# A retention layer with an MLP mixer on one core: another reserve behind crossbar turns, and another order of operations and loads

## The chip, the core and the metric

The kernel runs on one core of a Trainium2 chip. The core has five engines that run side by side, each with its own queue of instructions in fixed order: TensorE (PE in the profile; PEld is its loading of weights), VectorE (DVE), ScalarE (ACT), GpSimd (POOL) and SyncE (SP). Data goes between the device's memory (DRAM) and the core's memory (SBUF) by DMA, which POOL, SP and ACT issue; matmuls write into eight banks of accumulators (PSUM). The metric is the time of one execution on the device in microseconds (us).

## The reference

Two layers follow each other. For 4 batches, 8 heads, 768 steps and a head width of 64, a state decays by a factor of its head at each step and takes in an outer product; the output reads it with q. Then an MLP mixes along the steps, and another along the channels:

```python
def _attn_ref(q, k, v):
    gamma = 1.0 - 2.0 ** (-5.0 - np.arange(H))
    for t in range(S):
        state = gamma[None, :, None, None] * state + np.einsum('bhd,bhe->bhde', k[:, :, t], v[:, :, t])
        y[:, :, t] = scale * np.einsum('bhd,bhde->bhe', q[:, :, t], state)

def _moe_ref(x, w_tok1, w_tok2, w_ch1, w_ch2):
    xt = x.transpose(0, 2, 1)
    h = np.maximum(xt @ w_tok1, 0.0) @ w_tok2
    u = x + h.transpose(0, 2, 1)
    h2 = np.maximum(u @ w_ch1, 0.0) @ w_ch2
    return u + h2
```

x is the first layer's output with the heads side by side, (4, 768, 512). w_tok1 is 768 x 256, w_tok2 256 x 768, w_ch1 512 x 1536, w_ch2 1536 x 512. The output is float32.

## The kernel before

The recurrence is computed in six chunks of 128 steps: inside a chunk by masked score products, between chunks by a state that is carried on. The work falls into a front for each batch b and each of its four pairs of heads p, and a back for each batch.

**Front (function `front`).** q, k and v of a pair are loaded by POOL with a cast to float16 (the first k comes by SP in float32). k, and in batches 2 and 3 also q, is scaled with the head's decay (`decayed`, L533 on ACT or L535 on DVE, in two halves). Then both are turned, so that the head's width lies on the partitions (`turn`). A table named TURNS says how, for k, q and the result u: in batches 0 and 1 by PE (L557 for q, L559 for k, L792 for u) with a copy out of the bank by ACT or DVE; in batches 2 and 3 by the crossbar, which is a DMA with transpose that SP issues (L547 for k and q, L782 for u). After the turns, PE forms the chunk states (L589), which DVE carries on (L599, L601) and ACT scales (L619); it forms the scores (L640), which fill four banks and which DVE masks (L650); and it multiplies them with v (L670) and the states with q (L696). ACT casts the result (L712), PE runs the first MLP with the weights wt1 (L727) and wt2 (L747) with a relu between (L736 on ACT or L738 on DVE), and ACT casts u and keeps a float32 copy X (L712).

**Back (functions `widen`, `widen7`, `narrow`, `narrow7`).** With the turned u of all four pairs (the tile uT) and the weights wc1, PE forms the wide products. In batches 0 and 1 `widen` does it in a plain way (L826), with a relu by ACT alone (L842). In batches 2 and 3 `widen7` uses seven products in place of eight (L895), with sums of u (L865), copies (L906) and adds (L915); its six blocks begin with the products p1 and p2, which are the first to need uT. Then the narrow products with wc2 (L1044 and L1054 in the scheme of seven, L970 in the plain one) go through copies (L1034) and adds to X (L1061, L979), and the rows of X go out by a DMA that SP or ACT issues (L1087, L985).

**What sets the order.** Nothing is issued in the order of the source. All steps are recorded as `Op`s with the engines that they may run on, a planned cost for each and their dependences; `arrange` then plays the whole program through with those costs, a model of the DMA queues (`Rings`), the eight banks and the numbers of buffers. When an engine is free, it takes the first operation in its list that is ready. The list's order is given by `PRECEDENCE`, a string of two letters for each operation, found by a search outside of the kernel. The instructions are then emitted in the planned order, each engine's queue for itself; semaphores hold back whatever is early. Loads are requested in the order of the list `ORDER` at the end of the function (q00 is q of batch 0, pair 0; t1 and t2 are wt1 and wt2, a0 to a3 the pieces of wc1, b0 to b2 those of wc2), all on POOL's queue and at most a few at a time.

An operation may carry a guard. It counts in one place of `arrange`, where the time is worked out at which an operation may start:

```python
                x += (25 if eng[d.n] == e and d.dma is None else SEM) + o.guard
```

d is what the operation waits for and x is d's planned end. So a guard is a reserve in the plan alone: the operation is planned at least that many nanoseconds after the end of what it depends on, and so other work is planned ahead of it. No instruction comes of it. Before the change, every matmul step of the fronts of batches 1 to 3 has a guard of 200, and the steps of the back have none.

In the first 21 us of the plan, PE's holes of over 400 ns are partly filled with matmuls of zeros (fillers, L1164), as many as 0.7 of the planned hole divided by 165 ns (240 ns in the first two microseconds).

Of the kernel before, what the change touches and what calls it, by code (L numbers as in the profile page):

```python
# [89 lines left out]
def arrange(ops, BUFS, BANKS, rank):  # L90
# [181 lines left out]


PRECEDENCE = (
    "0b0900040a0105070c020d03060e080f230g272428250h260i382i373i2h330j2l342k2j350k2m29362n2a2o2b0l533m543h2c0m5543"
    "2d44560n472e3l3j2f453k2g460o393n482p2q3o2r0p3a492s3b4a3c3d4b4c3e4d4h3f0q4e4k574f4j3g0r2t584g3q4n2u4p3p4i4r3r"
    "4l0s2v4m3s5i2y2w3t5l2z0t2x5m593u31305a4o0u5b634q643v324s5h3w5c3y0v5k4t3x5d3z5j650w4u5e854066675f86415g5o0x5n"
    "4y7273425p765q4v5r68740y5s694w755t4z6a0z6b4x6c5u516d5077105v526h946e5y5w95116fhp5x6l5zhs6j6g12616khm606i62hj"
    "6n6mhnhkhqhthl6o6p13id6qighrihhuie146ri7iii8ifiaibi96shoicja81jb151z82i1i46ti52083i66x84hv21hwhy16hx22hz6ui0"
    "j46vi26ziy6wij6yiki317j570jjiljdje71jljkj8jcizj7jmjf7gj6181vj0iminj9is7jioit197hb0kb7iiuiv7kip1wiqa2jga3jh1x"  # L280
    "iwir7mji7l1y78ixjn1akc8779joju7a1b887b9089j17cjvj2911cjs7d8aj38b7ejp8c1dk5jtjy7fjqk78djw1ejz8eb17ojr7n8fk6jx"
    "7p968hk17q8j9z928ikga0k28g93k47rk0a1ax8l8nkr8k7s8mk9k8ay1fa4978o7wkska7tkt1gbva5k3khke7u98b28pku1hkk7va6997x"
    "a78qkdazkfkl7yki9abwa89bkv8ra9bxkjaa9c8skmab9ekw8vkp9g8tknct9f9h8wl09dko9i9j8xkqkx7z8u80cu9ll2kyl1kzadacl39k"
    "ah9n9ml6af9o8yael4cvl78zagaiakl59paml8ajal9q1ib3anlbc1byb49ub59rc21jbzb6aoc3b79sc4c0b8l99vc5c6ap9w9xla9tmqat"
    "lc9ybbaqc7benab9bdnbm1arbcm2c8bfm3ldasbgleaumsbacwmdawmeavmtcxbimmlfmncymfbhbjmpbk1klvmublma1lmrmblwmcmy1mlx"
    "mzn1ncn7n01nczmon2d0n8d1n31obmd2n9d3lsd4bnmvd5m7drboltd6dsm8dtbrlulpbplym9lzbqmjm0mwdumkd7mxmllqdblgepd8m4bs"
    "lmd9lrlnbudabtm5dclodec9m6dvddcanjeqcbdwlhdgccdfn4licdevdhernkceescgn5ewexcfcicheyn61pdxezljcjf0dyoretdz1qe0"
    "f1lke1ckosf2eue21rmgllmhclndnhe31sminfcpnicmnee41tdinlcnngnm1ucqolcoo5csomdjcrnoonnnoodko6opdlnpnqdmoqe5nrot"
    "oue6e9nse8dne7gloyntdoowgmovnudqnvdpoxfqf3nzoznxeafrecf4gnp3fno0p0fof7fseef6ebedgoo3f5efp4f9fbgpo1f8p6faego4"
    "p1fcnwo2ftfdnygreho7o8fugsgqfvelgtfwo9eigufxoap7fggyofpbp5oifjfhejfpgvocekp8emobfeodpaeoenoegwfffyp9gxohfzp2"  # L290
    "ogpcg1okfipsg5ojfkpgg4ptpdfmq9flg3puphg2pxg0pjpvqqpypepipkpwq0pfpzplq1pqpmpnq2prpoq7g7q4q8q3qbppqaq5qsr7qcqr"
    "qeq6g6qdqvqfqtqxqwqhsxquqgqig8qygaroqjqzqoqkg9qlr0qpr5gbqmr2r6ter9r1qnr8rer3rvrarcrprqr4rbrdrtrrgcrursrfgdrw"
    "rgs9rxrhrmrys3rnrjrirzs4gigerkghgfthtdggrls0tftjtigkgjs1svtgtms2tkgzs5tnsbtlsah3tqh0h1trh2tosys7h4h6h5tph7h8"
    "sgs6h9sctss8hashtttvsdhbtusetwhcsrtysksfssswhfsthdt0szheslt2hgsut1hihhsit3t4sjt6smt5snspt7t9t8tztbu3tauku4u0"
    "umtculu5u1u8u2upu9uauntxuqvpsoubu7ussqu6xqucurutuoviuduiuuv3ujufueuvuwugv1vzuxvjvkuhuzv2uyvlvnv0v6v4vow1vmwi"
    "v7v5vqv9vrv8vawgvsvxvbvgvyvuvtvcvhvdvvwny5vew0w6vwwhvfydw2w4wlwjw5y6w3wmwkytw7wow8x1wpw9wewqwvwfwbwawrwwwswc"
    "yuxnwty7wdwuy8xjy9wxxoyaxkx2xpxlxmxsyvxuwyxtwzx6x0xwxvx7xrxyybxxx8ycxzy1y0xax9y3y2xcy4xbx3xdywxeyxyyygyfxfx4"
    "xhyhyeyzx5z0xgyiypxiymylynyjyoyqykyrys"
)


# [1 line left out]
def kernel(  # L303
# [73 lines left out]
    def one(eng, cost, emit):  # L377
        return [(eng, cost[0], cost[1], emit)]
# [125 lines left out]
    def front(b, p):  # L504
# [22 lines left out]
        def decayed(tag, src, dep, g, hard):  # L527
# [12 lines left out]
            return dst, got  # L540
        K, kl = decayed("k16", KF, kd, gk, (b, p, "k") in HARD)

# [180 lines left out]
        def emit():  # L723
            acc = tile_of(T1, [P, 512], FP)
            for jt in range(NJ):
# [3 lines left out]
        t1 = op(one("PE", (672, 830), emit), x_ops + [wops["t1"], t2_done.get(b * NP + p - 1)],  # L729
                [T1], [X16])  # L730
# [11 lines left out]
        for j in range(2):  # L742
# [12 lines left out]
            t2 = op(one("PE", (335, 500), emit), [hr, wops["t2"], x_ops[j]], [], [H1, Y[j]])  # L755
# [50 lines left out]
    def back(b):  # L806
# [42 lines left out]
        def widen7():  # L849
# [3 lines left out]
            def u(k, half):  # L853
                return lambda: UT.tile[:, k * C2:(k + 1) * C2, half]
# [16 lines left out]
            def block(i):  # L871
# [6 lines left out]
                def weights(j):  # L878
                    if j < 4:
                        return lambda ct: AS.tile[:, j, ct, i * P:(i + 1) * P]  # L880
                    k, m = (j - 4) % 2, (j - 4) // 2
                    f = (i + m * M2) * P
                    return lambda ct: wc1[:, k * C2 + ct, f:f + P]

                def product(R, left, right, deps, first, extra):
                    opens = not lead

                    def emit():
                        if opens:
                            for x in H2s:  # L890
                                tile_of(x, [P, NF, SH], F16)
                        acc = tile_of(R, [P, 512], FP) if first else R.tile
                        r = right()
                        for ct in range(C2):
                            nc.tensor.matmul(acc[:, :SH], left(ct), r[:, ct], start=first and ct == 0,  # L895
                                             stop=ct == C2 - 1, skip_group_check=True)
# [200 lines left out]
        for f in steps:  # L1097
# [99 lines left out]
```

## Time and profile before

| what | value |
|---|---|
| time, median of 3 runs | 190.7 us (189.74 to 190.97) |
| the profiled execution | 190.58 us |
| its span, first to last instruction | 188.8 us |
| granted clock of TensorE | 1.0 |
| fillers (L1164) | 37 |
| crossbar turns on SP (L547, L782) | 24 |
| data moved by DMA | 24.92 MB |

The page's shares are averages over stages that have different limits: in the first 20 us the loads arrive one by one, later the engines limit each other. So the wait that ends last in a stage is looked for in that stage, by the timeline of an engine, by the table of busy times in stretches, and by the chain of waits, which goes back from the last instruction to what released each step. A row of the timeline gives start and length in us, the engine, the source line, the operation, the tiles and their shapes, how many instructions it merges, and in brackets the idle time ahead of it with what ended it. A matmul's length in such a row is longer than its share of PE's time, since matmuls overlap; the pace is read from the distance of starts.

### The profile page before, as it was taken

Reading aid. Unit: us, or ns where it says so; the run is one execution under the profiler, and the core shown is the slowest. Engines: PE = TensorE matmul, PEld = TensorE weight load, DVE = VectorE, ACT = ScalarE, POOL = GpSimd, SP = SyncE. Lnnn points to the kernel's source line nnn. Section 1 sums busy time; section 2 is a strip of 40 time slices with the busy share of each in tenths; the row PEclk is TensorE's granted clock in tenths of the full one; section 3 lists DMA queues with packets and bytes.
Section 4 is the critical chain, followed back from the end, with each engine's and each line's share of the span. In section 5 each row is a group of like instructions: output and inputs, shape, how many; then the busy total and the mean of one; then the engine's idle time right before and its main releaser. Section 6 shows DMA issues by size and latency. Waiting matters only on the chain.

```text
span 188.8 us, 5281 instructions
## 1 busy us (share of the span) xinstructions
PE 180.6 (96%) x2107; PEld 136.5 (72%) x2107; DVE 147.0 (78%) x398; ACT 145.7 (77%) x332; POOL 52.9 (28%) x62
## 2 busy tenths in 40 slices
PE   7977999999999999999899999999999999999993
PEld 3454898676688888866577988966678995656892
DVE  5588899455999988722078979989879978977972
ACT  7767899899979999999999979797884273766200
POOL 8995565634063604603016400000000000000000
PEclk9999999999999999999999999999999999999999
DMA  6999999999999999999999999683002044100044
GB/s 117 156 165 198 177 177 201 196 204 187 157 124 147 171 190 129 216 141 188 111 102 119 160 142 163 166 233 71 2 2 45 18 135 172 56 0 3 0 168 167
DMA packets 91977, 24.92 MB, mean 132 GB/s; under 512 B 81968, under 2 KB 89008, under 8 KB 91952
## 3 DMA queue, kind: packets, MB, share of 16 engines
q0 software_dynamic: 67456, 13.18, 92.0%
q1 hardware_dynamic: 24496, 11.41, 29.3%
q8 instruction: 16, 0.26, 0.7%
q14 instruction: 9, 0.07, 0.1%
HBM read 26.74 MB, written 6.29 MB: 175 GB/s over the span
## 4 chain that ended last, share of the span: by engine, by line
PE 73%; DMA 13%; ACT 5%; DVE 3%; POOL 3%; issue 1%; DVEq 0%; SPq 0%; POOLq 0%
PE bank L895 14%; PE bank L1044 13%; PE bank L826 11%; PE bank L1054 10%; DMA qT<-q 5%; PE bank L727 5%; PE bank L747 4%; DMA k<-in_k_dram 3%; PE bank L640 3%; PE bank L970 3%; PE bank L670 3%; DMA uT<-u 2%; PE bank L696 2%; PE bank L589 2%; DMA kT<-k 1%; PE bank L792 1%
## 5 line engine op out<-in xcount | busy, mean ns | idle before, releaser
L650 DVE TENSOR_TENSOR am<-bank,mask 128x384 f16<-128x384 f32 x64 | 32.0, 550 | 7.7 <-PE bank L640 7.7
L826 PE MATMUL bank<-uT,wc 128*128 128x384 f16 x192 | 35.6, 326 | 0.2 <-ACT X L712 0.2
L494 POOL DMA_DIRECT2D v<-in_v_dram x16 | 16.4, 1026 | 42.9 <-PE bank L696 19.6
L826 PEld LDWEIGHTS <-wc 128*128 128x128 f16 x192 | 17.7, 98 | 10.0 <-issue 0.5
L842 ACT ACTIVATE h<-bank 128x384 f16<-128x384 f32 x48 | 21.6, 518 | 1.5 <-PE bank L826 1.1
L1034 ACT COPY us<-bank 128x256 f32<-128x256 f32 x33 | 12.4, 381 | 12.8 <-PE bank L1044 12.7
L915 DVE TENSOR_TENSOR h<-bank,us 128x384 f16<-128x384 f32 x36 | 18.8, 552 | 4.3 <-ACT us L906 3.8
L906 ACT COPY us<-bank 128x384 f32<-128x384 f32 x36 | 16.4, 481 | 7.2 <-PE bank L895 5.2
L1044 PEld LDWEIGHTS <-hs 128*128 128x128 f16 x198 | 18.5, 98 | 2.3
L1061 DVE TENSOR_TENSOR X<-X,bank 128x256 f32<-128x256 f32 x44 | 17.8, 415 | 2.2 <-PE bank L1054 2.1
L619 ACT ACTIVATE cross<-U,gp 64x320 f16<-64x320 f32 x32 | 17.6, 560 | 2.5 <-DVE U L601 2.1
L1044 PE MATMUL bank<-wsum,hs 128*128 128x256 f16 x132 | 17.7, 273 | 0.0
L601 DVE SCALAR_TENSOR_TENSOR U<-U,gp,bank 128x64 f32<-128x64 f32 x64 | 16.2, 276 | 1.1 <-DVE U L599 0.2
L494 POOL DMA_DIRECT2D k<-in_k_dram x15 | 15.4, 1032 | 4.4 <-DMA wc<-in_moe_w_ch_dram 1.9
L712 ACT CAST x<-bank 128x384 f16<-128x384 f32 x32 | 14.8, 483 | 2.0 <-PE bank L696 1.9
L712 ACT CAST u<-bank 128x384 f16<-128x384 f32 x32 | 15.1, 488 | 1.1 <-PE bank L747 0.9
L533 ACT ACTIVATE k<-k,gk 128x384 f16<-128x384 f16 x24 | 14.3, 617 | 1.9 <-DMA k<-in_k_dram 1.8
L712 ACT COPY X<-bank 128x384 f32<-128x384 f32 x32 | 15.5, 496 | 0.1
L747 PE MATMUL bank<-h,wt 128*128 128x128 f16 x192 | 14.8, 219 | 0.0
L895 PE MATMUL bank<-hs,late 128*128 128x384 f16 x72 | 14.3, 326 | 0.0
L1054 PEld LDWEIGHTS <-h 128*128 128x128 f16 x132 | 12.7, 98 | 1.9
L1061 DVE TENSOR_TENSOR X<-X,us 128x256 f32<-128x256 f32 (+1 forms) x22 | 12.2, 554 | 2.4 <-ACT us L1034 1.9
(83 smaller groups left out, 355.3 us busy)
## 6 DMA issues: line engine op xcount, KB each, us to landing
out_dram<-X SPq DMA_DIRECT2D x23, 256.0 KB, 2.4
q<-in_q_dram POOLq DMA_DIRECT2D x16, 192.0 KB, 9.8
v<-in_v_dram POOLq DMA_DIRECT2D x16, 192.0 KB, 8.3
k<-in_k_dram POOLq DMA_DIRECT2D x15, 192.0 KB, 7.3
wc<-in_moe_w_ch_dram POOLq DMA_DIRECT2D x5, 512.0 KB, 13.5
wt<-in_moe_w_tok_dram POOLq DMA_DIRECT2D x2, 384.0 KB, 9.5
wc<-in_moe_w_ch_dram POOLq DMA_DIRECT2D x2, 256.0 KB, 9.2
us<-in_k_dram SPq DMA_DIRECT2D x1, 384.0 KB, 3.5
```

Source lines behind the costliest of these rows:

```text
L494: (nc.sync if hard else nc.gpsimd).dma_start(out=tile_of(s, [P, 2, NC, D], FP if hard else F16), in_=src.rearrange("h (c p) d -> p (h c) d ...
L619: nc.scalar.activation(r, u, AF.Copy, scale=g)
L650: nc.vector.tensor_tensor(am, SC[g].tile[:, :m * P].rearrange("p (i t) -> p i t", t=P), mask.to_broadcast([P, m, P]), ALU.mult)
L712: (nc.scalar.copy if e == "ACT" else nc.vector.tensor_copy)(tile(), t)
L747: nc.tensor.matmul(Y[j].tile[:, 2 * i * D:2 * (i + 1) * D], wt2[:, jt, t], H1.tile[:, jt], start=False, stop=(jt == NJ - 1), skip_group_ch ...
L826: nc.tensor.matmul(acc[:, :SH], wc1[:, ct, ft * P:(ft + 1) * P], UT.tile[:, ct, sh * SH:(sh + 1) * SH], start=(ct == 0), stop=(ct == NP - 1))
L842: nc.scalar.activation(H2.tile[:, ft], A.tile[:, :SH], AF.Relu)
L895: nc.tensor.matmul(acc[:, :SH], left(ct), r[:, ct], start=first and ct == 0, stop=ct == C2 - 1, skip_group_check=True)
L915: nc.vector.tensor_tensor(h(m, sh), R.tile[:, :SH], KS.tile[:, j], ALU.add)
L1044: nc.tensor.matmul(acc_[:, lo], l[:, j], r[:, j], start=first and j == 0, stop=j == K2 - 1, skip_group_check=True)
L1054: nc.tensor.matmul(acc_[:, lo], l[:, j], r[:, j], start=first and j == 0, stop=j == K2 - 1, skip_group_check=True)
L1061: (nc.vector if e == "DVE" else nc.gpsimd).tensor_tensor(dst(), dst(), b_(), ALU.add)
```

## The change

A constant RESERVE = (1500, 900) is added. The score products (L640) of the pairs whose q is turned by the crossbar, which are those of batches 2 and 3, get a guard of 1500 in place of 200. The products p1 and p2 of the first block of `widen7`, in batches 2 and 3, get a guard of 900 in place of none. PRECEDENCE is another string in the whole, and ORDER another list of loads. Computation, tiles, buffers, banks and the ways of turning are the same.

```diff
@@ PRECEDENCE @@
-    "0b0900040a0105070c020d03060e080f230g272428250h260i382i373i2h330j2l342k2j350k2m29362n2a2o2b0l533m543h2c0m5543"
...
+    "0f0j4f0e0c24272q250h2j2826373801032sa40b05070g00040d0a08092302064d0i29492l2k0k2m2n2o2a2b350l44362c452d0m3h46"
...
@@ before the operations are recorded @@
+    RESERVE = (1500, 900)
     HARD = {(0, 0, "k")}
@@ front: the scores @@
             a2 = op(one("PE", (k_, k_ + 155), lambda f=emit, r=run: f(r)), [kt, qt, two_before],
                     [SC[g] for g in run], [KT, QT], tiled="high")
+            a2.guard = RESERVE[0] if TURN[b, p, "q"] == "x" else a2.guard
             score_ops.update({g: a2 for g in run})
@@ widen7: block i @@
                 p2 = product(R3, weights(5), u(1, lo), ready + cw, True, [UT])
+                p1.guard = p2.guard = RESERVE[1] if i == 0 else 0
                 out_of(R3, 0, p2, k1, 0, 0)
@@ the loads @@
-    ORDER = ("q00 k00 q01 k01 v00 k03 k02 q02 v01 v02 q03 t1 t2 v03 k10 q12 q10 k11 v10 q11 q13 a1 a0 a3 "
-             "k12 a2 b1 b2 b0 q21 q20 v11 v12 k13 v20 v21 v13 k20 k21 k22 k23 v22 q22 q23 v23 k30 v30 q30 "
+    ORDER = ("q00 k00 q01 v00 k01 k02 k03 v01 v02 q02 q03 t1 t2 v03 k10 q12 q10 k11 q13 q11 a0 v10 a1 v11 "
+             "a3 a2 b1 b2 b0 k12 v12 k13 v20 v13 k20 q20 q21 v21 k21 k22 k23 v22 q22 q23 v23 k30 v30 q30 "
              "k31 v31 q31 v33 v32 k33 q32 k32 q33").split()
```

In the built program the counts of instructions change in a few places, by the planner's choice between engines: PE has 34 fillers for 37; ACT has 42 instructions of L533 for 41 and 16 of L736 for 15, and 5 copies of L572 for 6; DVE has 6 of L535 for 7, none of L738 for one, and 3 of L572 for 2; three output transfers of L1087 are issued by ACT instead of SP, 19 stay on SP for 22. The source lines from the score products on are one to three higher than before.

More of the change, by code (lines that the diff above doesn't have):

```diff
@@ L274 @@
 PRECEDENCE = (
-    "0b0900040a0105070c020d03060e080f230g272428250h260i382i373i2h330j2l342k2j350k2m29362n2a2o2b0l533m543h2c0m5543"
[L276 to L298, printed above, removed]
+    "0f0j4f0e0c24272q250h2j2826373801032sa40b05070g00040d0a08092302064d0i29492l2k0k2m2n2o2a2b350l44362c452d0m3h46"
@@ new lines @@
+    "3i3j54433m2e532f0n473f392g343k553a3l564e3n5m483b3c2r3o332h2i4a3d2u4p4b0q3e4c0o3g4h2p3q0p4k574j3r0r584g2t3s4n"
+    "4r5i0s2v5l2w4i2z4m0t2x4l593t3u315a2y5b634q4o640u3v324s5h403w3y5c0w5j4t5f5d3z5k650v5s4u5ohm5e4130665n3x4y425g"
+    "850x677273865p5r4v3p5q0y74684w504z755t0z164x95515u76946h521077625vhj5w6k5y115x6jhs5z6l606i126169hp6a6b6m136n"
+    "6chqht6dhnhk6ehlij6f797aikimhr7b7cin1h6g14ip7diqho6ohu6pi7iljejd6qi8ioidirie156rig1zhvifhwi9ia207eibhx6s217f"
+    "ici122jfi26tiyi3iz6xj06u787g6v17i47i6wi56y7jihi6hy7khz6z7h70iij1i07m71j2181vjnj3jjis19ja811w7lj482j51xjojb1a"
@@ new lines @@
+    "j67njgjc1y837piv841biwjljpixjk9087jm1cit9188jhjqiu7o89j7jrjij81d8a7qkb8bj98cjs8dk51e9zjukck6jt8e8fk77rjwjva2"
+    "8ha3jy7uk8jx8jb08ik1jz7sb18gkga0k28la1k08kk48m921faxkh8nk9kray7tkt93kkksaz7wku8okvkaklb5b67vkdb2969e8p8wa5kw"
+    "97ke7x98a6bvk3998qa79i7ya89bl0kfa98raa9ckil19dbwbx8sab9akj9g8t7z9hac9fknl4l5ctkm9k8u9mkokpb38v80cu9jkq9lb41i"
+    "l99nkxb78xla8y9ob8kyb9kz8z9pl2l39ql6agcvbyah9rbz9ul7n69sc0aeajal9v9tl8c1c29w9xlbc39ybbc4aic5akbfljamlkc6bemd"
+    "anmebcc71jldbdaoc81kbhbjcwlemacx1l1gn4mbn5cyaplflcbaadll1mbgbiatbkm1m2mc1nmjblmkm31om7mlm8aqm9lsarmfafltmnau"
@@ new lines @@
+    "msasbmawluavn2bnmmdrbodzezcmdhn3brdsn1czmomtdtd0bplvlmd1mud2bqd3lzd4bslpd5mylybtlwm0mzlglxlhd6duc9d7lilqcbn0"
+    "m4lndvcam5lrccdwn7locdepn8ewm6eqbumvcfd9chmwn9erd8njesmxdaceetdb1pmpnanecgdddccinhng1qcjdfnknfmqninb1rmrnleu"
+    "ckevnc1scldxdeexo5nddgeydy1tf0e0cne1f11uo6noe2nnmge3npf2nqnmmhe4cpnrnsmicodiolcqntopcscrongloromgmnunvdjgnfq"
+    "oooso3frdknwoqnxoynzdnfnnye5otdlo0oufso4e9dmo8e7ove8dodpe6fof3oxo2ozf5gop0gpf6dqeaf7ecp3f4eeebedpkftf9p4efo7"
+    "fbo1fpp6grp1egfuf8gsfvfap2ehocfzfwp5gtfdeifxguelfyodgqp7fcoaejgvp9ohekgwemfeobo9gxoieop8ffoeenpaogokg1ofpxpb"
@@ new lines @@
+    "fjg4ojgypupspcg5ptfhpgg3pifgpvphg0fkpdg2pjfmpypwflpzpeg7q0fipfqbplpqq1q9pmprpnq3q7poqsowq8q4q2ppqaqqq5qxqeqc"
+    "qrg9qgq6qfqdqvqtqhg6r9qiqyr7g8qoqkgaqlr0qpr5qmr2gbrer1r6qnror3r8rqrcr4rprarggch6rrrtrbgdrsrfrus9rwrhtwhcrirx"
+    "rvrmrnrjrdrys3svrkqws4qurzs0rltdgetotjs1teghggtfgisrthgjgfgktktistgztpswh3tms2tsh0tnh1sxh2tqtgh4sytrtth7yyh8"
+    "t2szqjqzh9tltvtuhat3txs5sbsshbsat6s6schfs7tyt0hds8sehgsdt1hisghesut4hhshsit5h5v4ukt8sjt9tbsfslsnsmtzspu3sou4"
+    "t7u0u5skulumu1u8upu9uasqu2uqunuru6ubustaucvku7tcuoutudv8v1uuuzufuev0uvuwugviv3uxv2vpuhuivjuyv6ujvnvlv7wgv5w1"
@@ L299 @@
+    "vowtv9vqvawivrw6vgvbvsvxvhvdvcvtvyx3wxxoxkxpx2vmwywzx6x4vuvevzwnvvydvfyew0vwylwjwlymw4w2wmy5wkw5w3wow8y6wpw7"
+    "xiwhxnwqwrwvw9wewwwswawfyiwbx1wcy7ynwuwdyoxjypyqxtxlx8xsx0x7xqx9xaxwyvxrxxyrx5xcysxbxmxyxuxdxfxey1xvxhxgy2y8"
+    "y4xzy9y0yaykyzz0yfy3ybyhygycyjytywyxyu"
 )
```

## The prediction

> **What bounds the kernel now.** I read the page first, for the engines' shares.
>
> ```profile
> span 188.8 us, 5281 instructions
> PE 180.6 (96%) x2107; PEld 136.5 (72%) x2107; DVE 147.0 (78%) x398; ACT 145.7 (77%) x332; POOL 52.9 (28%) x62
> ```
>
> TensorE (PE) is busy 96% of the span, so only 188.8 - 180.6 = 8.2 us are open to view, and a new order can win little more than PE's waits and the filler matmuls of the start. The profiled execution took 190.58 us, 1.8 more than its span and 0.1 below the median of the three runs, 190.7; all sums below are made against 190.58.
>
> Next the waits, of PE alone, and then the chain of waits around the three that belong to crossbar turns (start us, length us, what).
>
> ```profile
> PE bank L640 <- ACT h L842: 0.8, 1, 0.8
> PE bank L640 <- DMA kT<-k: 0.4, 1, 0.4
> PE bank L895 <- DMA uT<-u: 0.3, 1, 0.3
> PE bank L826 <- ACT X L712: 0.2, 1, 0.2
> ```
>
> ```profile
> 83.33 0.61 ACT q L533
> 83.98 10.03 DMA qT<-q
> 94.04 0.48 ACT h L842
> 94.56 0.51 PE bank L640 x12
> ...
> 121.85 2.83 DMA kT<-k
> 124.72 0.51 PE bank L640 x12
> ...
> 153.29 4.63 DMA uT<-u
> 158.05 0.57 DVE hs L865
> 158.66 9.60 PE bank L895 x58
> ```
>
> Two score products (L640) and the first wide product of the last batch (L895) stand until a turn has landed. How long, the timeline of PE tells with the pace of its matmuls, which the chain gives where PE runs unbroken.
>
> ```profile
> 36.68 2.60 PE bank L826 x16
> 65.79 1.31 PE bank L1044 x12
> 60.68 0.67 PE bank L727 x12
> ```
>
> ```profile
> 91.62 2.11 PE L826 MATMUL bank<-uT,wc 128*128 128x384 f16 x12
> 123.81 0.50 PE L747 MATMUL bank<-h,wt 128*128 128x128 f16 x6
> 156.74 0.98 PE L895 MATMUL bank<-uT,wc 128*128 128x384 f16 x5
> 157.97 0.65 PE L895 MATMUL bank<-uT,wc 128*128 128x384 f16 x3 [0.25 <-DMA uT<-u]
> ```
>
> A matmul of 384 columns takes 2.60 / 16 = 0.1625 us, of 256 columns 1.31 / 12 = 0.109, of 128 columns 0.67 / 12 = 0.056. So PE was done at 91.62 + 12 x 0.1625 = 93.57 and began the scores at 94.56: about **0.9** lost after 0.1 for the hand-over. At 123.81 + 6 x 0.056 = 124.15 against 124.72, by the same count: **0.45**. At 156.74 + 5 x 0.1625 = 157.55 against 157.97: 0.4; and at 157.97 + 3 x 0.1625 = 158.46 against 158.66: 0.2; together **0.6**. The three come to 1.95 us.
>
> The first is not the turn's alone. The turn lands at 84.0 + 10.0 = 94.0 to 94.4, while the bank comes from ScalarE's (ACT's) relu, 94.04 + 0.48 = 94.52. The table by stretches (PE, PEld, DVE, ACT, POOL busy) shows why:
>
> ```profile
> 60.00:70.00 10.00, 10.00 (x149) 8.99 (x147) 9.65 (x29) 9.96 (x26) 3.03 (x3) 1.00 1.79 178
> 84.00:90.00 6.00, 6.00 (x62) 3.95 (x60) 1.58 (x6) 5.87 (x16) 2.02 (x2) 1.00 1.61 194
> 90.00:95.00 5.00, 4.17 (x43) 2.68 (x41) 0.00 (x0) 4.93 (x12) 0.00 (x0) 1.00 3.29 112
> ```
>
> ACT has no free time around 60 to 95, and in the five us that hold the longest wait VectorE (DVE) has nothing to do. There ACT is the bound, whatever the turn does.
>
> **The change part by part.** The reserve itself issues nothing: it makes the planner start a score or a first wide product later after its turn, so that other matmuls go first. The built program has the same matmuls, but 34 fillers for 37. What moves is order.
>
> *Turn of kT before the scores at 124.7.* The rows of SP's timeline and of ACT's:
>
> ```profile
> 118.69 3.11 SPq L547 DMA_TRANSPOSE qT<-q  x1
> 114.33 1.12 ACT L533 ACTIVATE k<-k,gk 128x384 f16<-128x384 f16 x2
> ```
>
> The decayed k was ready at 114.33 + 1.12 = 115.45, but its turn was issued at 121.85, behind a q turn that took 3.11 to issue and that another, later score product needs. In the new order of SP that q turn stands behind it, and between the last result that ACT needs before this decay and the scores PE has 54 matmuls of 256 columns and 46 of 128: 54 x 0.109 + 46 x 0.056 = 8.5 us, and small ones beside them. ACT's three operations (under 2 us) and a turn of 2.8, as on the last row of the chain for kT, fit. Value -0.45; ends 0 and -0.45.
>
> *Last uT turn.* Between the product whose cast is turned and the first L895 there stood 42 matmuls of 256 columns; now 48. That is 6 x 0.109 = 0.65 more cover against 0.6 lost. SP has two outputs ahead of it as before. Value -0.5, as the turn of 4.63 may vary; ends 0 and -0.6.
>
> *Scores at 94.6.* Their q turn now stands in front of the uT turn on SP. PE has 72 matmuls of 384 columns and 53 of 128 between the relu that stands three places ahead of the q decay on ACT and the scores: 72 x 0.1625 + 53 x 0.056 = 14.7 us, enough for ACT's 2 and a turn of 10.4. So the turn is no longer late. What is late next is ACT. From the 24th to the 40th relu of the wide step (L842) ACT had 12 decays (L533) and 14 of L619; now 16 and 12, and one output transfer is issued from ACT instead of SP, while PE's work in that stretch is 0.2 us less.
>
> ```profile
> L533 ACT ACTIVATE k<-k,gk 128x384 f16<-128x384 f16 x24 | 14.3, 617 | 1.9 <-DMA k<-in_k_dram 1.8
> L619 ACT ACTIVATE cross<-U,gp 64x320 f16<-64x320 f32 x32 | 17.6, 560 | 2.5 <-DVE U L601 2.1
> 60.50 0.35 SPq L1087 DMA_DIRECT2D out_dram<-X  x1
> ```
>
> 4 x 14.3 / 24 - 2 x 17.6 / 32 + 0.35 = 2.4 - 1.1 + 0.35 = 1.6 us more on an engine with nothing to spare. Against that stands that the 24th relu comes 0.7 us earlier in PE's order. Ends: the 0.9 all gone, or replaced by 1.6, 0.7 worse. I take 0, in the middle.
>
> A row on turns, issue to landing over all 16 of L547 (and 10.0 is the one above):
>
> ```profile
> DMA to landing us min/median/max: 2.8/5.9/10.4
> ```
>
> The long ones fly beside the loads of POOL's queue, the short ones after those have ended. The Trainium skill (DMA: Bandwidth & Descriptors, "Queues, rings and completion order") has each DMA engine alternate, packet by packet, between the queue rows that have work. An estimate from it: one other row would make a turn of 2.8 last 5.6, the scores' turn would have landed at 89.6, and the 0.9 would be ACT's alone, so that the full gain below would shrink by 0.9 and its chance of beating 1% would be gone. The trace gives 3.7 times, not 2, and decides here.
>
> *Start.* The load of v00 moves ahead of k01, v01 and v02 ahead of q02; c1's first piece and v11 come earlier, v10, k12 and q20, q21 later; POOL's queue carries the same bytes ahead of wt2 as before.
>
> ```profile
> 8.39 1.12 ACT L533 ACTIVATE k<-k,gk 128x384 f16<-128x384 f16 x2 [0.55 <-DMA k<-in_k_dram]
> 11.20 0.61 ACT L533 ACTIVATE k<-k,gk 128x384 f16<-128x384 f16 x1 [0.29 <-DMA k<-in_k_dram]
> 10.96 0.51 PE L640 MATMUL bank<-qT,kT 64*128 64x128 f16 x12 [0.16 <-ACT kT L572]
> L473 POOL DMA_DIRECT2D wt<-in_moe_w_tok_dram x2: 769/834/898, 10.5 to 11.3; - x2
> DMA to landing us min/median/max: 9.0/9.5/10.0
> 21.50 0.83 PE L747 MATMUL bank<-h,wt 128*128 128x128 f16 x12
> ```
>
> k01 landed at 8.4 and the next k at 11.2, with v00 between them; moved behind v00, k01 lands in the middle, near 9.8, 1.4 later, and the scores of the second pair with it. But the first product with wt2 (L747) started at 21.50, when wt2 had just landed (11.3 + 10.0 = 21.3). From there on PE has work without a hole. wt2 keeps its place, so the start can win at most 0.2, and it loses only if the 1.4 is not made up by 21.3; in its favour DVE has one decay and one relu less to do, which ACT takes, and one copy of kT more. Value 0; ends -0.2 and +1.4. The three fillers dropped stood in holes: 0.
>
> *Rest of the new order.* Hand-overs that had time may now lack it. After 24 us the trace has waits of 0.2 to 0.8 in the list above; I take one more of 0.4, less the 0.2 of L826 that has lost its place: +0.2, ends -0.2 and +2.0 (all of 1.95 again elsewhere). The two other outputs moved to ACT come after 115 us, where the tail of the ACT-bound stretch is over: 0. The end is as it was, with a last product of 128 columns, one add and a small output.
>
> Sum: -0.45 - 0.5 + 0 + 0 + 0.2 = -0.75. 190.58 - 0.75 = **189.8 us**.
>
> **The rivals.** *The reserve works in full*: all 1.95 go, with the 0.2 of L826 and 0.2 at the start: 190.58 - 2.35 = 188.2. For it: covers that fit the turns everywhere. Against it: ACT's 4.93 of 5. *ACT takes over*: the 0.9 becomes 1.6, so 190.58 - 0.75 + 0.7 = 190.5, no change. For it: the count of decays. *ACT stands behind its output* (slower): the output issued on ACT waits for an add of DVE, and every relu, cast and decay is queued behind it, PE behind those for its banks. SP's outputs stood up to 1.3 for DVE:
>
> ```profile
> SPq L1087 <- DVE am L650: 2.5, 4, 1.3
> ```
>
> Then 1.6 + 1.3 = 2.9 stands for 0.9: 190.58 - 0.75 + 2.0 = 191.8. It decides from a wait of 0.75 on; against it, that one add may be done long before. *The start runs late*: 190.58 - 0.75 + 1.4 = 191.2, if the first L747 begins past 21.9. The *unnamed rest*, several new waits in the fresh order: 190.58 + 2.0 and more, 193.
>
> **How the numbers follow.** Forecast 0.42; reserve in full 0.15; ACT takes over 0.15; ACT behind its output 0.12; late start 0.10; rest 0.06. One per cent of 190.7 is 1.9, about what a measurement of this kernel can tell from no change, so faster means below 188.8 and slower above 192.6. Faster: 0.15 and 0.02 of the forecast's edge, 0.17. Slower: the rest and half of ACT's output, 0.06 + 0.06 = 0.12. Within: 0.71. The range goes from 188.3, just above the full gain, to 191.9, just above ACT's output; it leaves out some 0.1 on either side.
>
> **What would show it.** The scores that stood at 94.6 start without a wait on a DMA, and either with none (full gain) or with one on ACT's relu. The kT turn of the pair at 124.7 lands us before its scores. L895 of the last batch follows the matmul before it at once. First L747 near 21.5. ACT's output issue short, with no idle before the next ACT operation. The forecast is wrong if the first L747 moves by over 0.5, or if PE shows a wait above 1 us anywhere after 25.

## The result and the profile after

Over 20 runs each on one chip the changed kernel took 189.50 us in the median (189.18 to 190.41), the kernel before 190.34 (189.63 to 191.67): a ratio of 0.9957, 95% interval 0.9938 to 0.9977, that is 0.8 us less (0.4 to 1.2). The forecast was 0.75 less. The profiled execution of the changed kernel took 190.26 us, only 0.32 below that of the kernel before, and why it is so slow among its own runs is half of what follows. Its page begins:

```profile
span 188.5 us, 5267 instructions
PE 180.5 (96%) x2104; PEld 136.0 (72%) x2104; DVE 147.1 (78%) x397; ACT 144.6 (77%) x333; POOL 52.9 (28%) x62
```

TensorE is at 96% as before. The three longest rows of the list of what PE waited for (us in total, times, longest):

```profile
PE bank L1167 <- DVE zero L1158: 1.1, 1, 1.1
PE bank L590 <- DMA v<-in_v_dram: 1.0, 1, 1.0
PE bank L560 <- ACT k L534: 1.0, 1, 1.0
```

No crossbar turn stands in the whole list. (Lines have moved by one to three: L640 is L641 now, L747 L749, L826 L828, L842 L844, L895 L897, L1044 L1047, L1087 L1090.) The timeline of PE around the four places that the prediction named, and then SP's with the turns that belong to them (start us, length us, what):

```profile
22.31 0.84 PE L749 MATMUL bank<-h,wt 128*128 128x128 f16 x12 [0.54 <-DMA wt<-in_moe_w_tok_dram]
...
92.72 2.11 PE L828 MATMUL bank<-uT,wc 128*128 128x384 f16 x12
94.77 0.51 PE L641 MATMUL bank<-qT,kT 64*128 64x128 f16 x12
...
97.27 0.51 PE L641 MATMUL bank<-qT,kT 64*128 64x128 f16 x12
...
123.17 0.82 PE L1057 MATMUL bank<-wsum,h 128*128 128x256 f16 x6
123.92 0.51 PE L641 MATMUL bank<-qT,kT 64*128 64x128 f16 x12
...
155.62 1.47 PE L1047 MATMUL bank<-wc,hs 128*128 128x256 f16 x12
156.93 1.46 PE L897 MATMUL bank<-uT,wc 128*128 128x384 f16 x8
```

```profile
77.71 1.25 SPq L548 DMA_TRANSPOSE qT<-q  x1
...
83.66 1.22 SPq L548 DMA_TRANSPOSE qT<-q  x1
...
116.61 1.24 SPq L548 DMA_TRANSPOSE kT<-k  x1
...
152.44 1.22 SPq L784 DMA_TRANSPOSE uT<-u  x1
```

The scores at 94.77 follow on 92.72 + 12 x 0.1625 = 94.67, those at 123.92 on 123.17 + 6 x 0.109 = 123.82, the wide product at 156.93 on 155.62 + 12 x 0.109 = 156.93: each starts when PE is through with the work ahead of it. By the landings in the trace, the k turn issued at 116.61 landed at 119.41, 4.5 us ahead of its scores, the last uT turn at 155.18, 1.75 ahead. The three waits of 0.9, 0.45 and 0.6 are gone.

The scores at 94.77 are not the ones that stood at 94.56. In the built programs those were the scores of batch 2, pair 3; they come at 97.27 now, behind the scores of pair 2. In the kernel before it was the other way round, although the q turn of pair 2 landed first (78.38 + 9.8 = 88.2, against 94.4 for pair 3):

```profile
78.38 1.33 SPq L547 DMA_TRANSPOSE qT<-q  x1
```

```profile
97.35 0.51 PE L640 MATMUL bank<-qT,kT 64*128 64x128 f16 x12
```

In the changed kernel the two q turns, issued at 77.71 and 83.66, landed 11.0 and 7.8 us ahead of their scores. Even a turn of 10.4 would have been in time. No run swaps the two pairs alone.

Two losses stand against that. The first L749 starts at 22.31 in place of 21.50. And PE loses 1.5 us between 75 and 80, where the kernel before loses 0.3 (each matmul held against the median pace of its shape; most of it in gaps too short for the list of waits); in a second profile it is 1.2. ACT has no gap there. The chain of waits goes through ACT from 61.6 to 79.2:

```profile
61.13 0.42 DVE X L1064
61.63 0.38 ACTq L1090
...
78.42 0.77 ACT X L714 x2
79.23 0.32 PE bank L641 x5
```

ACT issues an output at 61.63 that had to wait for DVE's addition, and everything after it is ACT's own work. The table by stretches of the kernel before, and of the changed one (PE, PEld, DVE, ACT, POOL busy, then clock, DMA share, GB/s):

```profile
70.00:76.00 6.00, 6.00 (x110) 5.29 (x108) 4.60 (x13) 5.55 (x13) 2.50 (x3) 1.00 1.53 149
76.00:80.00 4.00, 4.00 (x64) 3.47 (x62) 3.14 (x12) 4.00 (x10) 2.57 (x3) 1.00 1.79 207
```

```profile
70.00:76.00 6.00, 5.96 (x94) 5.15 (x92) 4.82 (x15) 5.91 (x13) 2.03 (x2) 1.00 1.31 193
76.00:80.00 4.00, 3.81 (x64) 2.82 (x63) 3.93 (x11) 3.84 (x10) 0.00 (x0) 1.00 1.85 233
```

### The profile page after: what moved, and what is told of

It reads as the page before. It is cut to its first block, busy times and chain, and to the rows that moved or that the text cites. A ratio compares the mean times of both kernels' runs of the same rounds, so it can differ in the third digit from the quotient of the medians.

```text
span 188.5 us, 5267 instructions
## 1 busy us (share of the span) xinstructions
PE 180.5 (96%) x2104; PEld 136.0 (72%) x2104; DVE 147.1 (78%) x397; ACT 144.6 (77%) x333; POOL 52.9 (28%) x62
## 4 chain that ended last, share of the span: by engine, by line
PE 72%; ACT 11%; DMA 6%; POOL 6%; DVE 3%; issue 1%; ACTq 0%; POOLq 0%
PE bank L828 16%; PE bank L897 15%; PE bank L1047 12%; PE bank L1057 8%; DMA wt<-in_moe_w_tok_dram 6%; PE bank L749 5%; PE bank L729 4%; PE bank L973 3%; PE bank L641 2%; PE bank L672 2%; ACT k L534 2%; ACT cross L620 2%; POOL v L495 2%; POOL k L495 2%; PE bank L698 2%; POOL q L492 2%
## 5 line engine op out<-in xcount | busy, mean ns | idle before, releaser
L828 PE MATMUL bank<-uT,wc 128*128 128x384 f16 x192 | 36.1, 326 | 0.0
L828 PEld LDWEIGHTS <-wc 128*128 128x128 f16 x192 | 17.4, 98 | 9.2
L844 ACT ACTIVATE h<-bank 128x384 f16<-128x384 f32 x48 | 22.2, 508 | 0.6
L1047 PEld LDWEIGHTS <-hs 128*128 128x128 f16 x198 | 18.6, 98 | 2.6 <-issue 0.2
L534 ACT ACTIVATE k<-k,gk 128x384 f16<-128x384 f16 x25 | 14.8, 622 | 4.4 <-DMA k<-in_k_dram 3.3
L1047 PE MATMUL bank<-wsum,hs 128*128 128x256 f16 x132 | 17.3, 273 | 0.0
L749 PE MATMUL bank<-h,wt 128*128 128x128 f16 x192 | 14.8, 219 | 0.5 <-DMA wt<-in_moe_w_tok_dram 0.5
L897 PE MATMUL bank<-hs,late 128*128 128x384 f16 x72 | 15.1, 326 | 0.0
L749 PEld LDWEIGHTS <-wt 128*128 128x128 f16 x192 | 12.2, 98 | 2.3 <-DMA wt<-in_moe_w_tok_dram 0.7
```

The source lines that it names most:

```text
L534: nc.scalar.activation(t, src.tile[:, j], AF.Copy, scale=g[:, h:h + 1])
L749: nc.tensor.matmul(Y[j].tile[:, 2 * i * D:2 * (i + 1) * D], wt2[:, jt, t], H1.tile[:, jt], start=False, stop=(jt == NJ - 1), skip_group_ch ...
L828: nc.tensor.matmul(acc[:, :SH], wc1[:, ct, ft * P:(ft + 1) * P], UT.tile[:, ct, sh * SH:(sh + 1) * SH], start=(ct == 0), stop=(ct == NP - 1))
L844: nc.scalar.activation(H2.tile[:, ft], A.tile[:, :SH], AF.Relu)
L1047: nc.tensor.matmul(acc_[:, lo], l[:, j], r[:, j], start=first and j == 0, stop=j == K2 - 1, skip_group_check=True)
```

## The experiments

Edits that name operation numbers work on the finished plan, so that nothing else moves: `put(n, engine, ahead_of=m)` gives operation n to another engine, or moves it in the order of issue ahead of operation m. To set the start apart from the rest, this table has for each profile the start of the first product with the second weight block (first L747 or L749) and what is left of the span from there (span less that start). Fillers aside, the same 192 matmuls stand ahead of that product in every profile, so the rests can be compared.

| kernel | median us, ratio to before (95%) | span | first L749 | rest |
|---|---|---|---|---|
| before | 190.34 | 188.81 | 21.50 | 167.31 |
| changed | 189.50, 0.9957 (0.9938 to 0.9977) | 188.47 | 22.31 | 166.16 |
| changed, second time | 189.24, 0.9961 (0.9943 to 0.9979) | 187.27 | 21.27 | 166.00 |
| output on SP | 189.51, 0.9963 (0.9945 to 0.9980) | 187.03 | 21.25 | 165.78 |
| cross cleared first | 189.56, 0.9967 (0.9949 to 0.9985) | 187.53 | 21.19 | 166.34 |
| before, k turn first | 189.98, 0.9996 (0.9979 to 1.0014) | 188.69 | 21.79 | 166.90 |
| before, six fillers more | 190.44, 1.0017 (0.9993 to 1.0042) | 188.81 | 22.35 | 166.45 |
| changed, seven fillers more | 189.77, 0.9999 (0.9979 to 1.0019) | 188.93 | 22.94 | 165.99 |
| q decays on DVE | 190.03, 0.9996 (0.9974 to 1.0017) | 187.78 | 21.32 | 166.46 |
| four decays on DVE | 189.60, 0.9975 (0.9950 to 0.9999) | 188.79 | 22.24 | 166.56 |
| reserve alone | 193.39, 1.0163 (1.0143 to 1.0183) | 191.49 | 21.33 | 170.15 |
| search alone | 189.81, 0.9970 (0.9951 to 0.9989) | 188.22 | 21.62 | 166.60 |
| q decays in DVE's gap | 189.42, 0.9962 (0.9944 to 0.9981) | 187.11 | 21.63 | 165.48 |
| the same, mask first | 189.71, 0.9978 (0.9964 to 0.9991) | 188.44 | 22.76 | 165.68 |

The intervals are about 0.4% wide, 0.7 us; most edits here are worth less than that, so they are judged by the profile, matmul against matmul, and not by the medians.

**The changed kernel a second time**, no edit.

> The changed kernel as it is, for a second profile beside the three edits of this comparison. What is asked is whether its two losses repeat. Theory 'loads late': the transposed weight block of the third tile lands at 22.3 again and PE stands some 13.4 us of lost time behind at the first wide product, because the order of the loads and the memsets makes it so. Rival 'chance': that landing lies anywhere between 21.3 and 22.3 from run to run, and the second profile shows another value. The ACT stretch (PE losing about 0.9 us between 75 and 80) should repeat under both, since it hangs on the order of ACT's instructions. Time 189.5, 0.4% below the kernel before.

```profile
21.27 0.84 PE L749 MATMUL bank<-h,wt 128*128 128x128 f16 x12 [0.20 <-DMA wt<-in_moe_w_tok_dram]
```

The late start is not the program's: the block landed at 21.22 here and at 22.26 in the first profile, with the same bytes ahead of it and issues within 0.03 us of each other. The whole 1.05 us by which the first product is earlier, and 0.15 more, are still there at the last matmul. The loss between 75 and 80 came again.

**The output on SP.**

```diff
+    put(724, "SP", ahead_of=723)
```

> The changed kernel with one output of the first rows issued by SP instead of ACT, nothing else moved. Theory 'ACT behind its output': the output waits 0.83 us for DVE's addition and 0.38 us for its issue with all of ACT's queue behind it, ACT is then busy without a gap until 79 and PE loses 0.9 us at 75 to 80; without it ACT runs 1.2 us ahead and PE loses at most 0.1 there, so the time falls by 0.7 to 0.9 us against the changed kernel (about 188.7, ratio to the kernel before 0.991). Rival 'ACT's work': between 62 and 79 the work itself is what fills ACT, and the 1.2 us are used up by waits elsewhere on ACT; the loss at 75 to 80 stays above 0.6 and the time within 0.3 of the changed kernel's. Second rival: the output's landing on SP's queue pushes a crossbar turn back, and a wait on a turn shows on PE between 62 and 80.

ACT's row that follows in the place of the output:

```profile
60.55 1.12 ACT L534 ACTIVATE k<-k,gk 128x384 f16<-128x384 f16 x2 [0.35 <-DMA k<-in_k_dram]
```

These decays now wait 0.35 us for their load: they start at 60.55 in place of 61.04, so of an idle 0.82 and an issue of 0.38 only 0.49 came free. Against the second profile PE gains 0.33 by 75 and keeps 0.26 to the end; the stretch from 76 to 80 stays as it was (PE 3.80 of 4, ACT 3.82). The loss is ACT's work, not the output: the rival held.

**Clearing the cross tile first.**

```diff
+    order.insert(0, order.pop(at_))      # at_: where cross_op stands in the plan
```

> The changed kernel with DVE's clearing of the cross tile (1.0 us) back at the head of DVE's queue, where the kernel before had it, nothing else moved. Theory 'memset beside descriptors': while DVE clears the tile at 3.4 to 4.4, POOL's making of the first loads' descriptors is held back; moved ahead, the first load lands at 8.4 instead of 9.25, and the wait of L590 on it (1.0 us) shrinks by as much. Whether the end moves is a second question: if the lost start time is handed on, lost time at the first wide product falls from 13.4 to 12.5 and the time by 0.9; if the next loads catch up anyhow (the tile transposes' second block landed at the same 19.5 in both kernels), the end moves by less than 0.2. Rival 'order of loads': the first load is late because a v block and not a k block goes first; it lands at 9.25 again and nothing changes.

From issue to landing of the first v load, in this run, in the second profile of the changed kernel and in the first:

```profile
DMA to landing us min/median/max: 5.4/5.4/5.4
```

```profile
DMA to landing us min/median/max: 5.2/5.2/5.2
```

```profile
DMA to landing us min/median/max: 6.2/6.2/6.2
```

The same 5.2 to 5.4 us come with the clearing early and late, 6.2 in one run; the theory falls, and so does its rival (v first is not late as such). An effect smaller than the spread would not be seen: with the late clearing that load took 5.2 to 6.2 us in the nine profiles that have it. The Trainium skill (SBUF — State Buffer, "SBUF: two separate sides") tells of DVE operations in a two-port mode that keep GpSimd from writing descriptors. Nothing of it shows here: with 1.0 us of clearing beside the descriptors the load landed no later. Whether this clearing runs in such a mode, no run shows.

**The k turn first, in the kernel before.**

```diff
+    put(565, ahead_of=602)
```

> The kernel before with one edit: of the two crossbar turns that feed the scores at 124.7, the k turn is issued on SP ahead of the q turn instead of behind it, nothing else moved. Theory of the prediction: the k turn then lands well ahead of its scores and the 0.45 us of lost time at 124.7 go, all of it at the end too, since no later wait rose in that place: the time falls by 0.3 to 0.45 (ratio 0.998). Rival: the q turn, now second, lands as late as the k turn did, the wait changes its name and the time stays within 0.1 of the kernel before.

```profile
94.37 0.51 PE L640 MATMUL bank<-qT,kT 64*128 64x128 f16 x12
...
123.88 0.50 PE L747 MATMUL bank<-h,wt 128*128 128x128 f16 x6
124.31 0.51 PE L640 MATMUL bank<-qT,kT 64*128 64x128 f16 x12
```

```profile
118.62 1.26 SPq L547 DMA_TRANSPOSE kT<-k  x1
119.99 1.52 SPq L547 DMA_TRANSPOSE qT<-q  x1
```

123.88 + 6 x 0.056 = 124.22, and the scores follow at 124.31: the wait is gone. But the order need not be the only reason. The issue of the q turn on SP took 1.52 us here and 3.11 in the profile before. By an estimate from these rows a k turn behind it would have been issued near 120.2 and landed near 123.0, in time as well. Against the profile before, PE is 0.48 us further there than ahead of the wait; 0.2 is given back at 128.1, so 0.27 is kept there and 0.1 to 0.2 at the end, and the median's 0.2 less can't be told from none. What was not expected: the other scores, at 94.37, don't wait either, with nothing changed for them.

**More fillers at the start, in both kernels.**

```diff
+        if o.n == 103:                   # the first product with the second weight block
+            for _ in range(6):           # 7 in the changed kernel
+                nc.tensor.matmul(spare[:, :384], zero[:, :P], zero, start=True, stop=True)
         way[3]()
```

> The kernel before with six more filler matmuls of 384 columns (6 x 0.1625 = 0.98 us) on PE ahead of its first product with the third tile's second weight block, at 21.5; they write a bank that nobody reads. They put PE 1.0 us behind there, as a late landing of that weight block does. Theory 'the turn waits are slack': the turns at 94.6 and 124.7 land at times that hang little on PE's pace, so PE's delay is paid out of the waits of 0.9 and 0.45; by 130 PE is less than 0.3 behind and the time rises by 0 to 0.3 (ratio below 1.002). Rival 'everything shifts': turns are issued by results that PE's delay pushes along, the waits stay as long, and the time rises by 0.9 to 1.0 (ratio 1.005).

> The changed kernel with seven more filler matmuls of 384 columns (7 x 0.1625 = 1.14 us, 0.2 of it in place of a wait, 0.9 to 1.0 net) ahead of the same product at 21.3. Theory 'the turn waits are slack': the changed kernel has none of these waits, so the delay goes through to the end undiminished: the time rises by 0.9 to 1.0 against the changed kernel (median from about 189.35 to 190.3, equal to the kernel before within 0.3). Rival: ACT, which is short of time at 62 to 80, runs on its own and the delay is absorbed there by up to 0.8: the time rises by 0.2 only (189.5).

The kernel before, with six fillers:

```profile
22.35 0.84 PE L747 MATMUL bank<-h,wt 128*128 128x128 f16 x12
...
94.78 0.51 PE L640 MATMUL bank<-qT,kT 64*128 64x128 f16 x12
```

The block landed late here too, at 22.31, while the fillers ran. PE is 0.85 late at the first product, 1.11 at 72, 0.22 at these scores, 0 at the scores of 124.7 and 0.02 at the end: the span is the same to 0.01 us. The changed kernel, with seven:

```profile
22.94 0.83 PE L749 MATMUL bank<-h,wt 128*128 128x128 f16 x12
```

It is 1.66 late here (the fillers, and a weight block that landed 0.8 late) and 1.65 or 1.66 late at every matmul from here to the end: rest 165.99 against 166.00. The time rose by 0.0017 in ratio in the kernel before and by 0.0038 (0.9999 for 0.9961) in the changed one, in the direction of the theory, but the intervals overlap. In the profiles the delay is made up where the waits on turns were in the one, and passes through whole in the other. But part of why is another than I thought. The q turn that the scores at 94.56 had stood on, here:

```profile
L547 SPq DMA_TRANSPOSE qT<-q x1: 1219/1219/1219, 85.1 to 85.1; - x1
DMA to landing us min/median/max: 6.1/6.1/6.1
```

It took 6.1 us and landed at 91.2, where the profile of before has 10.4 and the run with the k turn first 7.8. So the wait was not of a fixed end that PE's delay moved towards; the turn was quick this time and there was no wait to pay out of. The wait at 124.7 went in the same way: the k turn still stood behind the q turn, but the issue of that took 1.89, and the k turn landed at 123.9, before PE was through with the work ahead (124.6).

The same rows settle who PE waited for at 94.56. ACT in this run, and in the kernel before:

```profile
94.07 0.53 ACT L842 ACTIVATE h<-bank 128x384 f16<-128x384 f32 x1
94.62 0.61 ACT L533 ACTIVATE q<-q,gy 128x384 f16<-128x384 f16 x1
```

```profile
92.95 0.54 ACT L842 ACTIVATE h<-bank 128x384 f16<-128x384 f32 x1
...
94.04 0.85 ACT L842 ACTIVATE h<-bank 128x384 f16<-128x384 f32 x2
```

With the fillers the scores started at 94.78, before the relu behind the q decay of 94.62 can have begun. In the profile of before that relu is the one at 94.04, to which the list had put the wait of 0.8. The scores never needed it; the last relu that they could need ended at 92.95 + 0.54 = 93.5. They waited for the turn alone.

**The decays at 75.5 on DVE**, and then with the output on SP and two decays of k.

```diff
+    put(430, "DVE")
+    put(431, "DVE")
```

```diff
+    put(724, "SP", ahead_of=723)
+    for n in (427, 430, 431, 461):
+        put(n, "DVE")
```

> The changed kernel with the two decays of q at 75.5 (1.12 us) issued by DVE instead of ACT; DVE idles 0.91 us just ahead of its masks there, so two decays of 0.31 should fit. Theory 'ACT's work' (held up by the run without ACT's output, which gained no more than 0.3): ACT has no gap from 62 to 80 and PE loses 0.8 to 1.0 at 75 to 80 waiting for its copies; with 1.1 us less on ACT ahead of 77 the loss falls to 0.2 or less, and as no wait follows it the time falls by 0.6 to 0.8 against the changed kernel (profile 188.3, median 188.7). Rival 'DVE is next': DVE is busy 4.9 of the 5 us from 75 to 80; its masks come 0.3 to 0.6 later, PE waits for them instead, and the time stays within 0.2.

> The changed kernel with that output on SP, the two decays of q at 75.5 and the two first decays of k at 65.1 and 70.2 on DVE: 0.4 + 4 x 0.6 = 2.7 us less on ACT between 60 and 77, 4 x 0.31 = 1.2 more on DVE, which idles 1.08 at 67.8 and 0.91 at 74.9. Theory 'ACT's work': PE's loss between 70 and 80 goes altogether, the time falls by 0.8 to 1.1 against the changed kernel (profile 188.1, median 188.4, ratio to the kernel before 0.991). Rival 'DVE is next': DVE's sums of the gated rows come later by up to 1.2 and PE waits for their banks; the time is that of the changed kernel or up to 0.5 above.

PE in the first of them:

```profile
78.73 0.34 PE L672 MATMUL bank<-v,am 128*128 128x64 f16 x6 [0.33 <-DVE am L652]
80.02 1.14 PE L828 MATMUL bank<-uT,wc 128*128 128x384 f16 x6 [0.19 <-DVE am L652]
```

Up to 77.4 PE gains 0.34 in the first and 0.66 in the second, by ACT's relief; by 79.6 it has lost 0.49 and 0.58 again, waiting for masks. The decays had landed behind the first mask in DVE's order, not in its gap, and pushed all the masks after it back. The rival held, in both. The second also lost 0.7 at 112, where ACT stood on one of the last loads:

```profile
109.61 1.12 ACT L534 ACTIVATE k<-k,gk 128x384 f16<-128x384 f16 x2 [0.61 <-DMA k<-in_k_dram]
```

That wait is 0 in the second profile of the changed kernel and 0.61 here, with that part of the program unchanged: a second place where the landing of a load decides.

**The reserve alone, the search alone.**

```diff
 # kernel before, with
+            a2.guard = RESERVE[0] if TURN[b, p, "q"] == "x" else a2.guard
+                p1.guard = p2.guard = RESERVE[1] if i == 0 else 0
```

```diff
 # changed kernel, without
-            a2.guard = RESERVE[0] if TURN[b, p, "q"] == "x" else a2.guard
-                p1.guard = p2.guard = RESERVE[1] if i == 0 else 0
```

> The kernel before with the two lines of the reserve alone: order of precedence and of the loads as before, the plan made again from them. Theory 'the reserve is what removes the waits': no scores and no first wide product stand on a turn any more (slack of 1.5 and 0.9 us), and as the order was not searched for it, other engines' results are waited for instead: the waits on turns fall from 1.95 to under 0.3, the time comes out between 0.3 below and 1.5 above the kernel before. Rival 'the search alone': the reserve does little, two of the three waits on turns are still there and the time is within 0.3 of the kernel before.

> The changed kernel without the two lines of the reserve: the new orders of precedence and of the loads, the plan made again from them. Theory 'the reserve is what removes the waits': scores come earlier than their turns again, PE stands 0.5 to 2 us in all on turns, and the time is 0.3 to 1.5 us above the changed kernel's. Rival 'the search alone': the new order keeps turns early by itself, PE has no wait on a turn, and the time is within 0.3 of the changed kernel's (ratio to before 0.996).

With the reserve alone 3.1 us are lost, twice the most that was expected. Waits of PE, and the stretches of the kernel before and then of this one:

```profile
PE bank L828 <- ACT h L844: 0.6, 2, 0.4
PE bank L897 <- DMA uT<-u: 0.5, 1, 0.5
```

```profile
60.00:76.00 16.00, 16.00 (x255) 14.29 (x253) 14.25 (x40) 15.51 (x38) 5.53 (x6) 1.00 1.69 168
76.00:95.00 19.00, 17.96 (x192) 12.36 (x189) 5.99 (x21) 18.68 (x44) 4.59 (x5) 1.00 2.14 160
```

```profile
60.00:76.00 16.00, 15.50 (x219) 13.61 (x218) 13.06 (x36) 14.40 (x34) 5.06 (x5) 1.00 1.79 175
76.00:95.00 19.00, 18.04 (x210) 12.60 (x210) 6.89 (x23) 18.73 (x44) 5.06 (x5) 1.00 1.72 164
```

No scores stand on a turn any more; the last uT turn is still waited for, 0.5. The plan puts other matmuls ahead, and from 60 to 76 ACT gets 1.1 us less to do than before, in front of a stretch in which it is full (18.7 of 19 in both); PE waits for ACT's relus, casts and copies instead. Between 22 and 175 us PE's busy time by stretches is 1.0 less than in the kernel before, of 2.84 by which the rest is longer; the others lie in gaps that the busy time does not show. Held against the median pace, PE loses 1.8 more than in the kernel before from 60 to 80, 0.5 more from 85 to 90 and 1.6 more from 95 to 165, and 1.0 less from 90 to 95, where the wait on the q turn was.

The search alone comes out 0.3 to 0.6 us above the medians of the changed kernel, inside the intervals. In its profile no matmul stands on a turn, and PE runs as in the changed kernel's second profile, 0.30 to 0.35 later from the start on; 0.6 more goes at 112, where ACT waits 0.53 for that late load again. So the new orders alone do what the profile shows. The reason is that the two programs are almost one: in the built programs all 2104 matmuls have the same order, and the two lines of reserve change two things. One mask stands three places later on DVE, and one output is issued by ACT, at 118.31, in place of SP, where without the reserve it stands ahead of the k turn for the scores at 123.9:

```profile
118.03 0.33 SPq L1088 DMA_DIRECT2D out_dram<-X  x1
118.45 1.38 SPq L548 DMA_TRANSPOSE kT<-k  x1
```

That turn landed at 123.25 here, 0.4 us ahead of its scores, in place of 4.5. So the reserve gives a margin at that one place, which this profile did not need. Which of the two orders, of operations or of loads, brings the gain, no run separates, and whether they would have been found without the reserve, this does not show.

**The decays in DVE's gap.**

```diff
+    put(724, "SP", ahead_of=723)
+    put(430, "DVE", ahead_of=376)
+    put(431, "DVE", ahead_of=376)
+    put(375, ahead_of=764)               # the second kernel alone
```

> The changed kernel with ACT's output at 60.5 issued by SP and the two decays of q at 75.5 on DVE, this time ahead of the masks at 74.9, in the 0.91 us in which DVE idles there, instead of behind the first of them. Theory 'two engines full at once': the loss of PE at 75 to 80 is ACT's as long as DVE's masks come no later; the decays now cost DVE nothing, so PE's wait for masks that the run with the decays among the masks showed (0.4 and 0.2) goes, and PE's loss in the stretch falls by 0.5 to 0.8 against the changed kernel: with an early start of the weight block a profile of 186.5 to 186.8, median 188.7 to 189.0. Rival 'masks bound': PE waits for masks again as soon as ACT runs ahead, and the gain stays under 0.3.

> As the run before it in this comparison (output on SP, decays of q on DVE in its gap), and one mask of DVE besides, the one at 77.3, put ahead of an addition of 0.68 us that nothing near waits for. Theory 'masks bound': where PE runs earlier than in the changed kernel, the masks decide next, and this one comes 0.6 earlier; the time falls by a further 0.2 to 0.4 against the run without it. Rival 'ACT alone': the masks have slack once the decays lie in the gap, the time is within 0.1 of the run without it; or the postponed addition frees a buffer late and PE waits for that, up to 0.3 above.

Stretches of the first:

```profile
70.00:76.00 6.00, 6.00 (x97) 5.31 (x95) 5.50 (x18) 5.45 (x12) 2.03 (x2) 1.00 1.22 254
76.00:80.00 4.00, 4.00 (x62) 2.72 (x60) 3.93 (x12) 3.69 (x8) 1.29 (x2) 1.00 1.90 193
```

PE is whole from 70 to 80, with no wait for masks: against the second profile of the changed kernel it goes from 0.38 behind at 60 to 0.26 ahead at 79.5. These 0.64 are the price of ACT's stretch, output included, as far as this edit reaches it, and the rest of 165.48 is the shortest of all. A mask moved forward as well brings nothing (165.68). No median shows the gain, because the start varies by more: the weight block landed at 21.58 and at 22.71 in these two.

## Why the prediction came out right

The sum was met, -0.75 forecast and -0.84 between the medians, but not by its terms. From the first product with the second weight block to the end the profiles gained 1.15 and 1.31; the forecast had 0.75 for that stretch.

- *kT turn, -0.45*: right for the profile; the turn now lands 4.5 us ahead. But the wait took two things, the old order on SP and an issue of 3.11 us for the q turn ahead. With the old order and an issue of 1.89 there was none, so on the average the term is worth less.
- *Last uT turn, -0.5*: right, and 0.6 in the profile. Beside the longer cover the turn itself was shorter, 2.7 from issue to landing for 4.6; with 4.6 it would have landed at 157.1, some 0.1 late, so either would have done nearly all of it. This is no chance: the turn took 4.5 to 4.9 in the three profiles with the old orders and in that of the reserve alone, where an output ahead of it on SP landed only after its issue and another was issued before it landed, and 2.7 to 2.8 in the ten with the new orders, where it flies between outputs. That the outputs make the difference fits all fourteen; no run moves them alone.
- *Scores at 94.6, value 0*: right as a sum, wrong in its reason. "There ACT is the bound, whatever the turn does" fails: the wait was the turn's alone, and all of the 0.9 went, since the pair whose turn landed first now goes first and both turns have 7.8 us and more to spare. ACT's work between the 24th and the 40th relu did grow, by 1.7 for the 1.6 of the sum, output included, and ACT did cost, at another place: 0.64 from 60 to 80 as far as the moved work shows, 0.3 of it the output's. I took the engine that the list names for a wait with two possible causes at its word.
- *Start, 0, if the block keeps its place*: the argument holds, the block landed at 21.2 in the second profile. But I took a landing of one run for a constant. In the fourteen profiles it landed between 21.0 and 22.7, at 22.0 or later in five: in one of four with the old order of loads, in four of ten with the new. The condition that the forecast is wrong if the first product moves by over 0.5 was met in the profiled run, and by chance.
- *Rest of the new order, +0.2*: the wrong sign, by some 0.4. No new wait of over 0.3 appeared after 25 us, and the 0.2 of L826 went.
- *ACT behind its output*, the rival on the slower side: it happened, with 0.83 idle and 0.38 issue, above the point of 0.75 from which it was to decide. Its price of 2.0 fell to 0.3, since the decays behind it would have waited for their load anyhow.
- *Full reserve*, 188.2: all its waits went. The lowest profiled time of the unedited changed kernel, with an early start, is 189.06; the 0.86 between is not far from ACT's 0.64, and with decays and output moved off ACT the rest is 0.5 shorter. The median, 189.50, lies 1.3 above.

How much the waits on turns are worth on the average, the profile of before overstates. Its turn of 10.4 us was one draw; two runs of nearly the same program show 7.8 and 6.1 and no wait at 94.6, and the one with the fillers had the 124.7 wait gone too, its rest only 0.3 to 0.45 above the changed kernel's. Only the wait on the last uT turn stood on a turn that was as long in every profile with the old orders. So part of the gain is that bad draws no longer count: the kernel before spreads over 2.0 us in 20 runs (189.63 to 191.67), the changed one over 1.2. That the turns make the upper half of that spread fits all profiles, but no run shows it for the timed runs, which have no trace. In the changed kernel two groups of times, up to 189.51 and from 189.80 on, fit an early and a late weight block; that is argued, not shown, in the same way.

## What to carry to other kernels

A wait seen in one profile may be a bad draw of a transfer: look at the transfer's length in a second profile before giving the wait a price. Where two products wait for two turns, look which turn lands first and whether its product goes first. Before crediting a new rule of the planner, plan the new orders without it and compare the two programs: here they differ in two places. Where a wait goes that stood late in a kernel, an earlier delay that it had hidden can come through whole, so the start is worth more afterwards. An engine that is full is relieved only if the work fits into a real gap of the other one, at the place in its order where that gap lies.

## What was not expected of the hardware

The same crossbar turn, issued at 84.0, 84.7 and 85.1 in three nearly equal programs, took 10.4, 7.8 and 6.1 us to land. The prediction's 5.6, an estimate from the Trainium skill's rule of alternating queue rows (DMA: Bandwidth & Descriptors, "Queues, rings and completion order"), is near the quickest of them; the traces show no constant factor. The two nearest loads were issued at the same distance from the turn in all three, 0.7 and 1.7 us after it. The last two were profiled on different chips and the chip of the first is not on record, so runs and chips are not told apart here. Loads on POOL's queue, issued at 11.23 to 11.27 us in the ten profiles with the new order, behind the same bytes, landed up to 1.6 us apart (21.14 to 22.71). On one chip alone it was 1.1 us (21.57 to 22.71 in three profiles).
